# Loading w2 two rows per partition, and reading w1's columns with a step of two

## The chip, the cores and the metric

The kernel runs on one core of one Trainium2 chip. The metric is the device time of one execution in microseconds (us). Several executions are timed; most of one kernel agree within about 1%, and now and then one is much longer at a lower granted TensorE clock. Such slow runs are left out of every ratio; the medians and ranges given below are over all runs of a kernel, slow ones included. A profile is one execution recorded by the hardware profiler. Its span is some 1.6 us shorter than the device time of the same run (167.6 against 169.21 us for the kernel before).

## The reference, cut to what matters

A sparse attention is followed by a mixture of experts with one expert for each batch entry.

```python
batch, n_heads, seq, head_dim = (4, 8, 768, 64)
B, S, D, E, F = (4, 768, 512, 8, 1024)
...
pooled = x.mean(axis=1)
e_idx = np.argmax(pooled @ w_gate, axis=1)
...
h = np.maximum(x[mask] @ w1[e], 0.0)      # w1[e]: 512 x 1024
out[mask] = gate_w * (h @ w2[e])          # w2[e]: 1024 x 512
```

Which expert a batch entry takes is known only when its attention is done. Then its w1 and w2 are loaded, as fp32 in HBM and bf16 in SBUF, while TensorE works on the attention of the next entry.

## The kernel before

The hidden dimension F = 1024 is cut into eight tiles `ft` of 128 columns of w1. Each tile is a 128-column weight load for each of the four row blocks `dt` of w1. w1 arrives in `CHUNKS[b]` pieces: four for batch entry 0, so that TensorE can begin when the first quarter of the columns has landed.

```python
CHUNKS = (4, 1, 4, 2)
...
sb["w1"] = moe_pool.tile([128, NDT, F], BF16, name="w1_sb")     # NDT = 4
sb["w2"] = moe_pool.tile([128, NFT, DM], BF16, name="w2_sb")    # NFT = 8
...
def w1f(c):
    fs = slice(c * F // CHUNKS[b], (c + 1) * F // CHUNKS[b])
    nc.gpsimd.dma_start(
        sb["w1"][:, :, fs],
        moe_w1[ds(sb["e"], 1)].rearrange("o (dt p) f -> p (o dt) f", p=128)[:, :, fs],
    )

def w2f():
    nc.gpsimd.dma_start(
        sb["w2"], moe_w2[ds(sb["e"], 1)].rearrange("o (ft p) d -> p (o ft) d", p=128)
    )
...
def h(ft, c0, c1):
    def mm():
        ...
        for dt in range(NDT):
            nc.tensor.matmul(
                ps["t"][:, 0 : c1 - c0],
                lhsT=sb["w1"][:, dt, ft * 128 : (ft + 1) * 128],
                rhs=sb["xT"][:, dt, c0:c1],
                start=(dt == 0), stop=(dt == NDT - 1),
            )
```

The order of instructions on each engine is worked out beforehand by the program's own scheduler from estimated durations.

The softmax here doesn't subtract the row's maximum and nothing guards it: scores larger than these inputs give would overflow.

## Time and profile before

| | kernel before |
|---|---|
| device time, median (range) | 169.25 us (168.56 to 172.78), 3 runs |
| profiled span | 167.6 us |
| TensorE busy | 158.1 us, 94% |
| mean granted clock | 1.000 |
| TensorE idle between 38 and 99 us | 3.2 us |

In the profile, PE is the TensorE matmul, PEld its weight load, POOL is GpSimd, ACT ScalarE and DVE VectorE. "L973" is a line of the kernel. In a timeline line, the bracket at the end is the idle time of that engine before the group, and what ended it.

### The profile page before, as it was taken

What the parts mean: (1) busy time and instruction counts of PE and PEld (TensorE: products, weight loads), DVE (VectorE), ACT (ScalarE), POOL (GpSimd) and SP (SyncE); (2) the same over time, 40 slices, a digit from 0 to 9 for tenths busy, and PEclk for the clock granted to TensorE, in tenths of its full rate; (3) what the DMA queues carried; (4) which work ended last, traced back from release to release, by engine and by line L of the source; (5) the groups of instructions that cost most, each with busy time, mean ns of one, the idle gap of its engine ahead of it and who ended that gap; (6) DMA issues with size and microseconds to landing.
All of it is one profiled execution on the core that took longest, in us unless ns stands there. A gap on an engine that the chain in (4) does not pass through costs nothing.

```text
span 167.6 us, 4958 instructions
## 1 busy us (share of the span) xinstructions
PE 158.1 (94%) x2085; PEld 91.2 (54%) x2085; DVE 99.6 (59%) x237; ACT 106.7 (64%) x196; POOL 63.7 (38%) x90
## 2 busy tenths in 40 slices
PE   6999999989899999899999889999999999999992
PEld 2446767745566564455666544555556544565451
DVE  5798785988996676799675787989542000000000
ACT  3455755476778889596877584559778534565342
POOL 6999937337940483951013893000002300000000
PEclk9999999999999999999999999999999999999999
DMA  4999999956999999699999999995300999900063
GB/s 100 204 235 223 176 247 215 188 101 82 150 198 206 243 217 194 105 207 272 233 261 246 216 199 199 221 242 161 132 2 4 142 185 200 348 4 0 11 241 125
DMA packets 24902, 29.06 MB, mean 173 GB/s; under 512 B 3856, under 2 KB 19472, under 8 KB 24880
## 3 DMA queue, kind: packets, MB, share of 16 engines
q0 software_dynamic: 18352, 20.58, 73.0%
q1 hardware_dynamic: 6528, 8.17, 15.8%
q8 instruction: 16, 0.26, 0.7%
q14 instruction: 6, 0.05, 0.1%
HBM read 35.67 MB, written 6.29 MB: 250 GB/s over the span
## 4 chain that ended last, share of the span: by engine, by line
PE 49%; DMA 26%; DVE 10%; issue 5%; POOL 4%; ACT 2%; POOLq 1%; ACTq 0%
DMA q_nat<-in_q_dram 13%; PE hps L1006 12%; PE hps L973 9%; DMA k_nat<-in_k_dram 8%; PE third L1006 7%; DMA v_f<-in_v_dram 5%; PE third L973 5%; DVE vblk L374 3%; PE sc L642 3%; PE ops L680 2%; PE ops L492 2%; PE tps L587 2%; PE sc L631 2%; PE third L1099 1%; DVE xs L706 1%
## 5 line engine op out<-in xcount | busy, mean ns | idle before, releaser
L263 POOL DMA_DIRECT2D v_f<-in_v_dram x30 | 25.2, 850 | 27.3 <-DMA w_sb<-in_moe_w_dram 19.6
L973 PE MATMUL hps<-xT_b,w_sb 128*128 128x512 bf16 (+1 forms) x172 | 33.3, 328 | 2.0 <-ACT hT_sb L984 1.5
L653 ACT ACTIVATE aT<-sc 128x768 bf16<-128x768 f32 x32 | 25.9, 810 | 14.2 <-PE sc L642 14.1
L973 PEld LDWEIGHTS <-w_sb 128*128 128x128 bf16 x256 | 23.1, 98 | 15.3 <-issue 1.5
L1006 PEld LDWEIGHTS <-hT_sb 128*128 128x128 bf16 x200 | 18.7, 98 | 19.9 <-issue 0.4
L1006 PE MATMUL hps<-w_sb,hT_sb 128*128 128x512 bf16 (+1 forms) x128 | 29.0, 373 | 0.2 <-ACT hT_sb L984 0.2
L984 ACT ACTIVATE hT_sb<-hps 128x512 bf16<-128x512 f32 (+1 forms) x43 | 20.2, 491 | 4.5 <-PE hps L973 4.3
L886 POOL DMA_DIRECT2D w_sb<-in_moe_w_dram x11 | 8.2, 753 | 31.8 <-PE hps L973 27.0
L1099 PE MATMUL third<-idle_in 128*128 128x512 bf16 (+3 forms) x61 | 17.0, 386 | 1.6 <-DVE warm L277 1.6
L1016 ACT ACTIVATE o_sb<-hps,gcol 128x512 f32<-128x512 f32 (+1 forms) x16 | 10.8, 673 | 10.3 <-PE hps L1006 9.3
L973 PE MATMUL third<-xT_b,w_sb 128*128 128x256 bf16 (+1 forms) x84 | 16.9, 324 | 0.0
L1006 PE MATMUL third<-w_sb,hT_sb 128*128 128x512 bf16 (+1 forms) x72 | 16.2, 368 | 0.0
L706 DVE TENSOR_TENSOR xs<-ops,rv 128x384 bf16<-128x384 f32 x28 | 15.6, 557 | 1.0
L724 ACT ACTIVATE xT_b<-tps 128x768 bf16<-128x768 bf16 x16 | 13.0, 810 | 3.2 <-PE tps L716 3.0
L657 DVE TENSOR_TENSOR aT<-aT,mask 120x768 bf16<-120x768 bf16 x22 | 12.0, 553 | 2.8 <-ACT aT L653 2.7
L581 DVE COPY kT<-kps 128x960 bf16<-128x960 bf16 (+1 forms) x18 | 12.7, 743 | 1.7 <-PE kps L561 1.7
L680 PEld LDWEIGHTS <-aT 120*64 120x64 bf16 (+1 forms) x384 | 8.7, 110 | 8.9 <-issue 5.0
L984 ACT ACTIVATE hT_sb<-third 128x256 bf16<-128x256 f32 (+1 forms) x21 | 10.1, 483 | 3.9 <-PE third L973 3.8
L705 DVE RECIPROCAL rv<-ops 128x6 f32<-128x6 f32 x28 | 5.4, 194 | 11.4 <-PE ops L680 8.9
L450 POOL CAST v_h<-v_f 128x768 bf16<-128x768 f32 x12 | 9.9, 836 | 5.9 <-DMA v_f<-in_v_dram 5.7
L1016 ACT ACTIVATE o_sb<-third,gcol 128x512 f32<-128x512 f32 (+1 forms) x9 | 6.0, 663 | 8.4 <-PE third L1006 8.4
L612 DVE TENSOR_REDUCE kmx<-kT 128x24 bf16<-128x768 bf16 x12 | 11.3, 939 | 0.0
(83 smaller groups left out, 209.5 us busy)
## 6 DMA issues: line engine op xcount, KB each, us to landing
out_dram<-o_sb SPq DMA_DIRECT2D x23, 256.0 KB, 5.1
v_f<-in_v_dram POOLq DMA_DIRECT2D x30, 192.0 KB, 9.7
w_sb<-in_moe_w_dram POOLq DMA_DIRECT2D x5, 1024.0 KB, 13.9
k_nat<-in_k_dram POOLq DMA_DIRECT2D x6, 384.0 KB, 8.4
q_nat<-in_q_dram POOLq DMA_DIRECT2D x6, 384.0 KB, 10.1
w_sb<-in_moe_w_dram POOLq DMA_DIRECT2D x8, 256.0 KB, 7.7
vblk<-vblk SPq DMA_DIRECT2D x12, 89.4 KB, 5.3
w_sb<-in_moe_w_dram POOLq DMA_DIRECT2D x2, 512.0 KB, 6.4
```

The lines of the kernel that those rows point to most:

```text
L263: eng.dma_start(v_f[:, :, h, :], v[b, h].rearrange("(j p) d -> p j d", p=128))
L581: nc.vector.tensor_copy(kdst, win)
L653: nc.scalar.activation(aT, sb["sc"][:, :, 0 : NH * QB], ACT.Exp, scale=SCALE)
L657: nc.vector.tensor_tensor(out=aT[0:NR], in0=aT[0:NR], in1=mask[:, hf * NH : (hf + 1) * NH, :] .rearrange("p j c -> p (j c)") .unsqueeze(1) ...
L680: nc.tensor.matmul(ops[(j % 2) * QB : (j % 2 + 1) * QB, hh, jj // 2, :], lhsT=aT[0:rows, hh, jj * QB : (jj + 1) * QB], rhs=vb[0:rows, pr, ...
L706: nc.vector.tensor_tensor(out=sb["xs"][pr][:, hf * NS : (hf + 1) * NS, :, :].rearrange("p s h d -> p h s d"), in0=ops[:, :, :, 0:D], in1=r ...
L724: nc.scalar.activation(sb["xT"][:, pr, :].rearrange("p (j e g) -> p j e g", e=QB // G, g=G), sb["xps"].rearrange("p j g e -> p j e g"), AC ...
L973: nc.tensor.matmul(ps["t"][:, 0 : c1 - c0], lhsT=sb["w1"][:, dt, ft * 128 : (ft + 1) * 128], rhs=sb["xT"][:, dt, c0:c1], start=(dt == 0), ...
L984: nc.scalar.activation(sb["hT"][:, ft, c0:c1], ps["t"][:, 0 : c1 - c0], ACT.Relu)
L1006: nc.tensor.matmul(ps["t"][:, 0:n], lhsT=sb["hT"][:, ft, st * 128 : (st + 1) * 128], rhs=sb["w2"][:, ft, c0:c1], start=(ft == 0), stop=(ft ...
L1016: nc.scalar.activation(ps["o"][:, 0:n], ps["t"][:, 0:n], ACT.Copy, scale=sb["gcol"][:, 0:1])
L1099: nc.tensor.matmul(idle[:, 0:c], lhsT=idle_in[:, 0:128], rhs=idle_in[:, 0:c], start=True, stop=True)
```

## The change

The intent is longer DMA packets. If a partition holds two neighbouring rows of w2, one packet covers 2 x 512 fp32 values, 4 KB, in place of 2 KB, and there are half as many. The rows then lie in another order over partitions, so the hidden units must too. Tile `ft` takes every second column of a block of 256 columns of w1.

```diff
         def w2f():
             nc.gpsimd.dma_start(
-                sb["w2"], moe_w2[ds(sb["e"], 1)].rearrange("o (ft p) d -> p (o ft) d", p=128)
+                sb["w2"].rearrange("p (c i) d -> p c (i d)", i=2),
+                moe_w2[ds(sb["e"], 1)].rearrange("o (c p i) d -> p (o c) (i d)", p=128, i=2),
             )
...
-                        lhsT=sb["w1"][:, dt, ft * 128 : (ft + 1) * 128],
+                        lhsT=sb["w1"][:, dt, ft // 2 * 256 : (ft // 2 + 1) * 256].rearrange(
+                            "p (f i) -> p i f", i=2
+                        )[:, ft % 2, :],
```

## The prediction

> **What bounds the kernel now.** I read the page's engine totals first, then the busy time of each engine by stretch, then the chain of work that ended last, then the few stretches in which TensorE stood still, and last the DMA traffic.
>
> ```profile
> PE 158.1 (94%) x2085; PEld 91.2 (54%) x2085; DVE 99.6 (59%) x237; ACT 106.7 (64%) x196; POOL 63.7 (38%) x90
> ...
> q0 software_dynamic: 18352, 20.58, 73.0%
> ```
>
> TensorE is busy 158.1 of 167.6 us, so 9.5 us are idle. By stretch (columns: window, its length, busy us and instructions of each engine, granted clock, DMA share, GB/s):
>
> ```profile
> 8.00:38.00 30.00, 28.77 (x546) 18.83 (x544) 25.21 (x59) 17.70 (x30) 19.95 (x28) 1.00 1.07 196
> 38.00:99.00 61.00, 57.82 (x916) 34.31 (x915) 47.96 (x108) 46.75 (x89) 32.04 (x41) 1.00 1.10 202
> 99.00:143.00 44.00, 44.00 (x476) 23.84 (x475) 21.13 (x50) 27.10 (x51) 5.21 (x7) 1.00 0.84 152
> ```
>
> The last row matters most: from 99 to 143 us TensorE never stops, so no earlier weight can help there; only work handed to it before 99 us can. Between 38 and 99 us it is idle for 3.2 us. The TensorE timeline shows where (start, us, what, idle before it and its releaser):
>
> ```profile
> 43.40 1.04 PE L973 MATMUL hps<-xT_b,w_sb 128*128 128x512 bf16 x4 [0.49 <-DMA w_sb<-in_moe_w_dram]
> ...
> 67.79 0.38 PE L909 MATMUL ops<-grec,ones_row 1*128 1x1 f32 x2 [1.15 <-DVE grec L906]
> ...
> 97.14 0.60 PE L973 MATMUL hps<-xT_b,w_sb 128*128 128x256 bf16 x4 [1.54 <-ACT hT_sb L984]
> ```
>
> The first is the first piece of w1 of batch 0, which the change does not move. The other two are what is at stake. The chain, in order of time, says what lies behind them (start, us, what):
>
> ```profile
> 42.60 13.38 DMA k_nat<-in_k_dram
> ...
> 56.27 8.53 DMA v_f<-in_v_dram
> ...
> 69.71 21.82 DMA q_nat<-in_q_dram
> ...
> 94.04 0.84 POOL v_h L450
> 94.91 0.85 ACT vblk L372
> 95.77 0.85 ACT vblk L372
> 96.62 0.48 ACT hT_sb L984
> ```
>
> It runs through GpSimd's DMA queue. In that queue w2 of batch 0 stands ahead of the k, q and v that batch 2 needs (the 13.38 us), and w2 of batch 1 ahead of those of batch 3 (the 21.82 us). v that lands late is cast late (POOL L450), the in-order ScalarE and VectorE sit in front of that cast (ACT L372; at 66 us DVE L374), and TensorE waits. So two of the four w2 transfers are on the path. The other two (batch 2 from about 106 us, batch 3 from about 138 us) lie beside a TensorE that is full; batch 3's w2 is first used near 154 us.
>
> **What the Trainium skill says.** "DMA: Bandwidth & Descriptors", section "Why small descriptors are slow (HBM only)": each packet pays a fixed cost of about three cycles, 27% at 256 bytes; longer packets pay it less often. Its section "Where 436 GB/s comes from" puts a ceiling of 435 GB/s on 16 engines. The trace agrees that little is left. w2 now moves as packets of 2,048 bytes of fp32 in, 1,024 of bf16 out; w1 of batch 1, loaded whole, already has the length that w2 would get, 4,096 in and 2,048 out. Two stretches in which each has the queue practically to itself:
>
> ```profile
> 48.50:51.50 3.00, 3.00 (x45) 2.04 (x44) 2.77 (x7) 2.16 (x6) 0.49 (x1) 1.00 1.24 209
> 71.50:72.50 1.00, 1.00 (x11) 0.34 (x10) 1.00 (x3) 0.95 (x4) 1.00 (x2) 1.00 1.18 211
> ```
>
> The last column counts bytes written: 209 GB/s for the short packets, 211 for the long. Read in fp32 that is 418 and 422 GB/s, both near the page's 435.
>
> "TensorE: Matmul & The Clock Gate", section "Weight-path perf modes": a weight load of 128 columns that are not fp32 is done in a fast mode, in four chunks of 32 columns "packed or strided", for column steps up to 1,024. A step of two should keep it. The trace shows that the mode is on (TensorE weight-load groups; the number after the comma is ns of one):
>
> ```profile
> L973 PEld LDWEIGHTS <-w_sb 128*128 128x128 bf16 x256 | 23.1, 98 | 15.3 <-issue 1.5 <-DMA w_sb<-in_moe_w_dram 0.6
> ...
> L680 PEld LDWEIGHTS <-aT 120*64 120x64 bf16 x288 | 6.5, 110 | 8.0 <-issue 4.9 <-DVE xs L706 1.3 <-DVE vblk L520 0.8
> ...
> L492 PEld LDWEIGHTS <-bind 64*32 64x32 bf16 x48 | 2.8, 92 | 0.5 <-issue 0.3
> ```
>
> 128 columns take 98 ns, less than the 110 ns of 64. No strided load is in this trace, so the step itself is untested here.
>
> **The change part by part.**
>
> 1. w2's packets. Each w2 has 128 x 8 = 1,024 packets now and 128 x 4 = 512 after; bytes are the same. Four transfers lose 4 x 512 = 2,048 packets. Time of one w2 alone on the queue: 1,048,576 bytes / 209 GB/s = 5.02 us now, / 211 = 4.97 us after: 0.05 us less. While output stores share the engines (part of batch 1's w2), the saving may be larger; I allow 0.05 to 0.25 us there. Two on the path: 0.1 to 0.3 us, I take 0.2.
>
> 2. Issue on GpSimd. A w1 issue with 512 packets takes 0.75 us and a w2 issue with 1,024 takes 0.90 us in the median (w2 rows of that line: 899/902/1067 ns). So w2 should come down to 0.75, 0.15 us less. But k, q and v behind it stand in a queue that is already full for 20 us, so this lies beside the transfer: I count 0.05 us on the path.
>
> 3. Room in the queue. GpSimd stands still before v's issues until earlier transfers land: 19.6 us in 5 waits for w_sb. Half as many packets should let it issue one or two v transfers earlier. They still run behind w2 in the same queue, and the last issues still wait for w2 and k to land, so the last v lands no earlier for it: 0.
>
> 4. w1's weights with a step of two: 256 loads in number as before. If the fast mode stays: 98 ns, 0. If it falls off: by the 92 and 110 ns above, one column costs (110 - 92)/32 = 0.56 ns, so 128 would take 110 + 64 x 0.56 = 146 ns (an estimate). The narrow matmuls of L973 (256 columns) follow each other at (0.60 - 0.273)/3 = 0.109 us, where 0.273 is the length of one. Transposes of 128 columns, each with its own 128-column load, go at
>
> ```profile
> 61.50 0.50 PE L716 MATMUL tps<-identb,xs 128*128 128x128 bf16 x6
> ```
>
> (0.50 - 0.22)/5 = 0.056 us with 98 ns loads, so loads overlap each other and their length is mostly latency. A slow load would add some 48 ns of it and still fit in 109: 0.
>
> 5. Nothing else: the moving operands, the order of instructions on each engine, PSUM and the evictions are as before (w2 sits in the tile in the same shape, with its rows permuted as hT's partitions are).
>
> Sum: 0.2 + 0.05 = 0.25 us less. 169.25 - 0.25 = 169.0 us.
>
> **Rivals.**
>
> - The per-packet cost counts in full. The records of single packets have a median of 60, 98 and 173 ns for 512, 1,024 and 2,048 written bytes: some 23 ns fixed. If packets ran one after the other, w2 would go from 1,024 x 98/16 = 6.27 us to 512 x 173/16 = 5.54 us, 0.74 less, 1.5 us for the two: 167.8 us. For it: both stalls (1.15 and 1.54 us) are large enough to give that. Against it: the DMA share of 1.24 says that packets overlap, and the rate of 209 against 211 GB/s is measured, not inferred.
> - The long packets overlap less or starve the output stores: w1 of batch 1 has a share of 1.18 instead of 1.24. If w2 came out 0.5 us longer each, the time would be about 170.0.
> - The strided load costs TensorE. If loads could not overlap and took 146 ns, the 128 narrow matmuls of L973 would each lose 146 - 109 = 37 ns: 4.7 us, all on a full TensorE, 174.0 us. The L716 spacing speaks against it; nothing in this trace rules out a load that is slow in throughput.
> - A larger gain is barred: both stalls gone entirely would be 1.15 + 1.54 = 2.7 us, 166.6 us or 1.6%, still short of 2%.
>
> **Range and chances.** The three earlier runs lie between 168.56 and 172.78, with the profiled one at 169.21, so most of the range is scatter around 169.0; the first rival stretches it down, the second up. 168.0 to 170.1 us. Faster by over 2% would need more than the two stalls: 0.01. Slower by over 2% needs the strided load to fail, or a slow draw: 0.04. Within 2%: 0.95.
>
> **What would show it.** The software queue should have 16,304 packets instead of 18,352 and the same 20.58 MB; its share falls, by the packet medians, by 4 x (6.27 - 5.54)/167.6 = 1.8 points to about 71.2%. w2's issue on GpSimd near 0.75 us. The waits of v's issues for w_sb in two or three pieces instead of five, with a similar sum. The loads of L973 at 98 ns, their matmuls still 0.109 and 0.217 us apart. The two stalls before L909 near 67 us and L973 near 97 us shorter by 0.1 to 0.3 us together, and TensorE without a gap from then to 143 us. I am wrong if L973's loads are over 110 ns and its matmuls spread, if a stall on w_sb appears where none was, or if a stall shrinks by a microsecond, which would mean that packets cost more than the rates show.

## More of the kernel before

The waits on semaphores (counters that a finished instruction or transfer raises and that others wait for) are not written in the program. The framework puts them in from what each instruction reads and writes.

## The result, and the profile after

The changed kernel took 173.99 us in the median of four runs (173.55 to 175.55), against 169.37 us for four runs of before. The ratio is 1.03, with a 95% interval of 1.0226 to 1.0374. Ratios here are the mean time of one kernel's fast runs over that of the other's from the same rounds, so they are not quite the ratio of the medians. The profiled run was the longest, 175.55 us with a span of 174.0; a second profile, e7 below, has 171.5.

The page after, with its busy time, the clock by slice, and the software queue:

```profile
PE 158.2 (91%) x2057; PEld 92.1 (53%) x2085; DVE 101.2 (58%) x237; ACT 106.9 (61%) x196; POOL 63.2 (36%) x90
...
PEclk9999999999957999999999999999999999999999
...
q0 software_dynamic: 16304, 20.58, 68.9%
```

TensorE is as busy as before (158.2 us), but the span is 6.3 us longer, so it stands still longer. In two slices near 50 us the granted clock is lower. The software queue moves the same 20.58 MB in 2,048 packets fewer, as intended. What TensorE waited for, after (us in total, times, longest):

```profile
PE hps L974 <- DMA w_sb<-in_moe_w_dram: 6.0, 1, 6.0
...
PE hps L974 <- ACT hT_sb L987: 1.3, 1, 1.3
```

Before, the same first row had 0.5 us. One wait for w1 or w2 is now 6 us long. The weight loads show where it starts (timeline of PEld after):

```profile
43.20 0.10 PEld L974 LDWEIGHTS <-w_sb 128*128 128x128 bf16 x1 [0.47 <-DMA w_sb<-in_moe_w_dram]
48.82 0.14 PEld L974 LDWEIGHTS <-w_sb 128*128 128x128 bf16 x2 [5.52 <-issue]
```

The first load of batch 0's first group, row block 0, goes at 43.20 us. The second, row block 1, comes 5.6 us later. The profile calls the idle time before it "issue", which means that it names no releaser. In the kernel before, all four loads of this group go together, the first two 15 ns apart (timeline of PEld before):

```profile
43.40 0.54 PEld L973 LDWEIGHTS <-w_sb 128*128 128x128 bf16 x4 [0.62 <-DMA w_sb<-in_moe_w_dram]
```

Each load has its matmul. The record of the group's first matmul is missing from the trace after, so that timeline has three:

```profile
48.85 1.44 PE L974 MATMUL hps<-xT_b,w_sb 128*128 128x512 bf16 x3 [5.98 <-DMA w_sb<-in_moe_w_dram]
```

The chain that ended last names the transfer (start, us, what):

```profile
40.77 7.95 DMA w_sb<-in_moe_w_dram
...
48.85 1.44 PE hps L974 x3
```

What was issued at 40.8 us is w1's fourth and last piece, and it landed at 48.7. The trace also has a new instruction on the queue of weight loads, one that only waits for semaphores (minimum, median, maximum ns; first and last start in us):

```profile
L974 PEldq EVENT_SEMAPHORE  x2: 51/51/51, 48.7 to 124.9; - x2
```

The one at 48.7 us waits for pieces three and four, and the second load itself for piece two. In the kernel before, the group waited for the first piece's semaphore alone. The one at 124.9 us belongs to batch 2; its pieces had landed by 117.1 us, so there the wider wait costs nothing. The waiting is followed by a slow stretch (window, length, busy us of the five engines, granted clock, DMA share, GB/s; after):

```profile
43.30:48.80 5.50, 0.00 (x0) 0.00 (x0) 2.54 (x4) 0.85 (x2) 3.81 (x5) 0.91 1.28 185
48.80:55.00 6.20, 6.15 (x52) 3.02 (x53) 2.54 (x5) 2.34 (x4) 1.65 (x2) 0.53 1.17 204
```

TensorE does nothing for 5.5 us and then runs at a mean clock of 0.53 until 55 us. The matmuls of 512 columns start 0.425 us apart in that stretch, where they start 0.216 apart otherwise. "TensorE: Matmul & The Clock Gate", section "Part 1: The HAM clock gate", says that the clock falls to one half after an idle window of about 3.4 us and comes back after a busy one. The long waits agree: the half clock runs from 47.85 to 54.67 us here and for 3.41 us in e7, each time after TensorE had stood still for the 3.4 us before. Other traces do not: in e1, e3, e6, e8 and e11 six stalls of 1.0 to 2.3 us were also followed by half clock (3.41 or 6.83 us of it), though TensorE was busy for 1.2 to 2.6 of the 3.4 us before the fall, while other stalls, up to the 1.8 us in e4, were not. What decides between these is not shown.

Both traces have 2,085 weight loads in the same order. The start of each one after, minus the start of the same one before, gives the account:

| place in the kernel before | shift after | shift e7 (second profile) |
|---|---|---|
| 42.5 us, before the first w1 group | -0.05 us | -0.37 us |
| 43.41 us, second load of that group | +5.41 | +4.38 |
| 55 us, clock back at full | +7.79 | +5.66 |
| 66 us | +7.80 | +5.66 |
| 70 us, past the old stall before L909 | +6.57 | +4.44 |
| 99 us, past the old stall before L973 | +6.34 | +3.91 |
| 164 us, last store's matmul | +6.35 | +3.92 |

The wait costs 5.5 us (4.7 in e7), the half clock another 2.4 (1.3). Of this 1.2 us come back at 67 us. The kernel before had stood still there for 1.15 us because v came late, and with TensorE itself late, v is no longer what it waits for. Another 0.2 to 0.5 us come back near 97 us. From 99 us on nothing changes.

### The profile page after: what moved, and what is told of

It is laid out like the page before. It is cut to its first block, busy times and chain, and to the rows that moved or that the text cites. A ratio compares the mean times of both kernels' runs of the same rounds, so it can differ in the third digit from the quotient of the medians.

```text
span 174.0 us, 4932 instructions
## 1 busy us (share of the span) xinstructions
PE 158.2 (91%) x2057; PEld 92.1 (53%) x2085; DVE 101.2 (58%) x237; ACT 106.9 (61%) x196; POOL 63.2 (36%) x90
## 3 DMA queue, kind: packets, MB, share of 16 engines
q0 software_dynamic: 16304, 20.58, 68.9%
## 4 chain that ended last, share of the span: by engine, by line
PE 55%; DMA 17%; DVE 15%; issue 5%; POOL 3%; ACT 2%; POOLq 1%; ACTq 0%
PE hps L974 14%; DMA q_nat<-in_q_dram 13%; PE hps L1009 12%; PE third L1009 6%; PE third L974 6%; DMA w_sb<-in_moe_w_dram 5%; PE ops L680 3%; PE sc L642 3%; DVE vblk L374 3%; DVE kT L581 2%; PE tps L716 2%; PE tps L587 2%; PE sc L631 2%; DVE xs L706 1%; DVE vblk L313 1%
## 5 line engine op out<-in xcount | busy, mean ns | idle before, releaser
L974 PE MATMUL hps<-xT_b,w_sb 128*128 128x512 bf16 (+1 forms) x164 | 34.3, 337 | 7.6 <-DMA w_sb<-in_moe_w_dram 6.0
L974 PEld LDWEIGHTS <-w_sb 128*128 128x128 bf16 x256 | 23.6, 100 | 21.4 <-issue 8.2
L263 POOL DMA_DIRECT2D v_f<-in_v_dram x30 | 25.4, 854 | 26.2 <-DMA w_sb<-in_moe_w_dram 17.5
L1009 PE MATMUL hps<-w_sb,hT_sb 128*128 128x512 bf16 (+1 forms) x121 | 28.4, 372 | 0.7 <-ACT hT_sb L987 0.2
L1009 PE MATMUL third<-w_sb,hT_sb 128*128 128x512 bf16 (+1 forms) x68 | 15.5, 367 | 0.4 <-issue 0.3
L657 DVE TENSOR_TENSOR aT<-aT,mask 120x768 bf16<-120x768 bf16 x22 | 12.8, 587 | 2.8 <-ACT aT L653 2.8
L642 PE MATMUL sc<-qT,kT 64*128 64x64 bf16 x384 | 11.5, 194 | 0.0
L642 PEld LDWEIGHTS <-kT 64*128 64x128 bf16 x384 | 7.6, 96 | 7.1 <-issue 5.3
```

The source lines that it names most:

```text
L263: eng.dma_start(v_f[:, :, h, :], v[b, h].rearrange("(j p) d -> p j d", p=128))
L642: nc.tensor.matmul(sc[:, hh, jj * QB : (jj + 1) * QB], lhsT=sb["kT"][pr][rs, j, :], rhs=sb["qT"][pr][rs, j, :], start=not add_shut, stop=n ...
L657: nc.vector.tensor_tensor(out=aT[0:NR], in0=aT[0:NR], in1=mask[:, hf * NH : (hf + 1) * NH, :] .rearrange("p j c -> p (j c)") .unsqueeze(1) ...
L974: nc.tensor.matmul(ps["t"][:, 0 : c1 - c0], lhsT=sb["w1"][:, dt, ft // 2 * 256 : (ft // 2 + 1) * 256].rearrange("p (f i) -> p i f", i=2)[: ...
L1009: nc.tensor.matmul(ps["t"][:, 0:n], lhsT=sb["hT"][:, ft, st * 128 : (st + 1) * 128], rhs=sb["w2"][:, ft, c0:c1], start=(ft == 0), stop=(ft ...
```

## The experiments

My theory after seeing the two traces was this. When the framework asks which transfers a read must wait for, it compares a contiguous read with each transfer's pieces exactly, but takes a strided view by its outer limits. Piece c of w1 covers columns 256c to 256c+255 of all four row blocks of 1,024 columns, so its outer limits run from 256c to 3,072 + 256c + 255. A strided read in row block 1 (1,024 to 1,278) lies within the outer limits of all four pieces. One in row block 0, columns 0 to 254, lies within those of the first piece only. The rivals were that strided weight loads are themselves slow, and that the long w2 packets hurt the queue.

e1, e6, e4 and e2 ran on one chip with five rounds, e3, e5 and e7 on one with three, and e8, e9 and e11 on another with three to five.

### e1: the change, with w1 stored piece by piece

```diff
+            sb["w1c"] = sb["w1"].rearrange("p dt f -> p (dt f)").rearrange(
+                "p (c dt f) -> p c dt f", c=CHUNKS[b], dt=NDT)
...
-                sb["w1"][:, :, fs],
+                sb["w1c"][:, c, :, :],
...
+                per = NFT // CHUNKS[b]
-                        lhsT=sb["w1"][:, dt, ft // 2 * 256 : (ft // 2 + 1) * 256].rearrange(
+                        lhsT=sb["w1c"][:, ft // per, dt, ft % per // 2 * 256 : (ft % per // 2 + 1) * 256].rearrange(
```

> The changed kernel with w1's tile stored piece by piece, so that each of batch 0's four w1 transfers fills one unbroken stretch of a partition; the strided weights and the long w2 packets stay. Theory (the wait): a strided view was taken to touch every transfer whose outer limits it crosses, so the second weight load waited for all four; here it crosses one only. The 5.5 us stall and the half clock after it go, the first L974 group runs near 43.2 us without a gap inside, clock 1.0, and the time is 168.6 to 169.6 us, ratio to before 0.995 to 1.002. Rival (strided loads themselves cost TensorE): it stays at 172 to 174. Rival (long w2 packets hurt the queue): it stays above 171. The sum of my prediction, a gain of 0.25 us, would show as 0.9985.

Measured: correct, 169.56 us median (168.81 to 170.25), ratio 1.0012 (0.995 to 1.0074). The loss is gone although every w1 load is strided and every w2 packet is long. The timeline of e1's TensorE:

```profile
44.60 0.81 PE L978 MATMUL hps<-xT_b,w_sb 128*128 128x512 bf16 x3 [0.16 <-issue]
```

There is no wait inside the group. It ran at 44.6 us, while the last packets of w1's fourth piece were written at 48.6. The profiled run reached this place 1 us late because of a 1.0 us stall at 31.7 us before attention matmuls, with 3.4 us of half clock after it (mean clock 0.99, where I had expected 1.0). Such a stall between 31 and 35 us is in the profiles of e1, e3, e5, e6, e8 and e11.

### e6: the kernel before, with w1 stored piece by piece

The same layout with contiguous weights and short w2 packets.

> The kernel before with the same piece-by-piece w1 tile, contiguous weights and short w2 packets: the control for e1. Theory: the kernel before did not suffer from the wait, so nothing changes, ratio 0.998 to 1.002. Rival: if the layout of the tile alone speeds w1's transfer or moves a wait, this differs from 1 as much as e1 does.

Measured: correct, 169.75 us (168.85 to 170.3), ratio 1.0023 (0.9958 to 1.0087). The ratio is just above the expected 1.002, and its interval includes 1. The layout by itself changes nothing that these runs resolve, so e1's recovery is not a gain of the layout that hides a loss of the stride.

### e4: w2's long packets alone

```diff
-                sb["w2"], moe_w2[ds(sb["e"], 1)].rearrange("o (ft p) d -> p (o ft) d", p=128)
+                sb["w2"].rearrange("p (c i) d -> p c (i d)", i=2),
+                moe_w2[ds(sb["e"], 1)].rearrange("o (c p i) d -> p (o c) (i d)", p=128, i=2),
```

> Wrong result on purpose: only w2's packets are two rows long, w1 is read as before, so w2's rows do not match the hidden units. Theory: no wait is added, ratio 0.996 to 1.001 (a gain of 0.1 to 0.3 us of 169), w2 issue 0.75 us, 16,304 packets. Rival (the fixed 23 ns of a packet count in full): 1.5 us less, ratio 0.991. Rival (long packets hurt): above 1.005.

Measured: wrong result; 169.37 us (168.79 to 171.63), ratio 0.9997 (0.9933 to 1.0061). The long packets neither hurt nor help the time measurably. The interval ends at 0.9933, so the 0.991 of the rival that counts each packet's fixed cost in full is outside it, if narrowly. The stretch in which batch 0's w2 has the queue to itself, e4:

```profile
48.50:51.50 3.00, 3.00 (x50) 2.03 (x46) 2.87 (x7) 2.16 (x5) 0.82 (x1) 1.00 1.13 214
```

It moves 214 GB/s where the kernel before moved 209, which would make one w2 of 1,048,576 bytes 0.12 us shorter (4.90 us in place of 5.02). But in the same window the other profiles have 212 with short packets (e6) and 213 (e1) and 210 (after) with long ones, so a gain of this size is not told from scatter.

### e2: one strided view added to the kernel before

```diff
                 ps["t"] = moe_bank(ps["n"])
+                if b == 0 and ft == 0 and c0 == 0:
+                    nc.tensor.matmul(
+                        ps["t"][:, 0:1],
+                        lhsT=sb["w1"][:, 1, 0:256].rearrange("p (f i) -> p i f", i=2)[:, 0, :],
+                        rhs=idle_in[:, 0:1], start=True, stop=True)
                 for dt in range(NDT):
```

> The kernel before plus one matmul of one column whose weights are a strided view of w1 of batch 0, row block 1, put ahead of the first group; everything else is contiguous, and the result is right because the group starts its sum afresh. Theory (the wait): this single strided view is enough to wait for all four w1 transfers; stall near 5.5 us at 43 us, half clock after it, total 173 to 174.5 us, ratio 1.022 to 1.037. Rival (the 256 strided loads cost): one load costs nothing, ratio 1.00.

Measured: correct, 175.16 us (173.89 to 176.96), ratio 1.0336 (1.0252 to 1.0419). The time is above the expected 173 to 174.5 us, the ratio within what was expected. One strided load out of 257 brings the whole loss:

```profile
48.55 0.16 PE L973 MATMUL hps<-idle_in,w_sb 128*128 128x1 bf16 x1 [5.93 <-DMA w_sb<-in_moe_w_dram]
```

### e8: the same, in row block 0

```diff
-                        lhsT=sb["w1"][:, 1, 0:256].rearrange("p (f i) -> p i f", i=2)[:, 0, :],
+                        lhsT=sb["w1"][:, 0, 0:256].rearrange("p (f i) -> p i f", i=2)[:, 0, :],
```

> As e2, but the strided one-column matmul reads row block 0 of w1 in place of row block 1. Theory (outer limits): block 0, columns 0 to 255, ends before the second transfer's first element, so its outer limits cross the first transfer alone; no wait is added, ratio 0.995 to 1.005. Rival (any strided view waits for every transfer into the tile): ratio 1.022 to 1.037 as e2.

Measured: correct, 169.43 us (167.99 to 171.91), ratio 0.9946 (0.9889 to 1.0004). The ratio is just under the expected 0.995 to 1.005, and far from the rival's. Its profile fell on a run of 171.91 us that counts as slow, so only its order of events is read:

```profile
44.67 0.18 PE L973 MATMUL hps<-idle_in,w_sb 128*128 128x1 bf16 x1
44.92 0.81 PE L981 MATMUL hps<-xT_b,w_sb 128*128 128x512 bf16 x3
```

The strided load and the group behind it wait for nothing, while w1's second, third and fourth pieces landed only at 47.4, 48.7 and 50.0 us. So it is not any strided view of the tile that waits for all transfers. It depends on where the view lies, as the outer limits say.

### e3: w1's step alone

The w1 part of the diff without the w2 part.

> Wrong result on purpose: only w1's columns are read with a step of two, w2 is loaded as before. Theory (the wait): the whole loss is here, ratio 1.022 to 1.037, the 5.5 us stall at 43 us. Rival (long w2 packets are the cause): ratio 1.00.

Measured: wrong result; 175.7 us (174.39 to 187.18), ratio 1.0333 (1.0241 to 1.0425). The whole loss belongs to the w1 half of the change. In the profiled run the wait was 4.2 us rather than 5.5, since that run came to the group 2.6 us late, after the stall at 32 us and the half clock that followed it.

### e5 and e7: work to do during the wait, and the change again

```diff
                 ps["t"] = moe_bank(ps["n"])
+                if b == 0 and ft == 0 and c0 == 0:
+                    for _ in range(26):
+                        nc.tensor.matmul(
+                            ps["t"], lhsT=idle_in[:, 0:128], rhs=idle_in, start=True, stop=True)
                 for dt in range(NDT):
```

> The changed kernel with 26 idle matmuls of 512 columns put ahead of batch 0's first w1 group, so that TensorE has work while it waits for all of w1. 26 x 0.216 us = 5.6 us, about the wait. Theory: the wait stays but the clock does not fall, so the 2.35 us that the half clock took between 48.8 and 55 us are saved: 171.2 to 172.2 us, ratio 1.010 to 1.020, mean clock 1.0. Rival (the clock falls for another reason, or the loss is elsewhere): as the changed kernel, 1.025 to 1.03.

> The changed kernel unaltered, on the same chip as the two others, for comparison: ratio 1.022 to 1.037, clock 0.98.

Measured: e5 was correct, 173.66 us (172.17 to 187.07, the last a slow run), ratio 1.0183 (1.0105 to 1.0262). e7 took 173.7 us (173.11 to 174.87), ratio 1.0274 (1.0205 to 1.0343). The ratio of e5 is within what was expected, but its median is not (nor is that of its three fast runs, 172.94), and the two intervals overlap, so the timing alone does not settle it. The trace of e5 does, in two windows, the wait and what follows:

```profile
44.90:50.30 5.40, 5.39 (x25) 2.45 (x25) 2.73 (x4) 1.13 (x2) 4.00 (x5) 1.00 1.29 189
50.30:56.00 5.70, 5.54 (x74) 3.21 (x74) 3.14 (x7) 3.74 (x8) 1.38 (x2) 1.00 1.17 205
```

The clock stays at 1.00. From the second load to 55 us the shift against before goes from +7.08 to +6.90, so nothing is added, where the changed kernel added 2.4 and e7 1.3 us. The fall of the clock is a consequence of the wait and costs 1.3 to 2.4 us, depending on the run.

### e9 and e11: batch 1's w2 issued behind batch 3's v

The stall at 97 us, which my prediction wanted to shorten, comes from v standing behind w2 in the queue. w2 is not needed so early, so I moved it.

```diff
-        w2 = add("POOL", 0.8, [], w2f, dma=6.3, after=w1[-1:])
+        if b in (1,):
+            w2 = lambda o: add("POOL", 0.8, [], w2f, dma=6.3, after=w1[-1:] + o)
+        else:
+            w2 = add("POOL", 0.8, [], w2f, dma=6.3, after=w1[-1:])
...
             vl, rest = load_next(nxt + 1, last_T[b], casts, order_pool)
+            if b in (1,):
+                ...
+                w = (w[0], w[1](order_pool[:]), w[2])
```

> e1 (changed kernel, w1 stored piece by piece) with batch 1's w2 issued behind batch 3's v instead of ahead of it. w2 of batch 1 is first used near 101 us and landed near 88; v of batch 3 landed near 95 and holds up TensorE for 1.2 to 1.5 us at 97. Expected if that stall is the queue's: v some 5 us earlier, stall gone, w2 landing near 95, ratio to before 0.990 to 0.996. Rival: the program's own scheduler orders the engines anew from the changed list, and what it gains there it loses elsewhere: 0.997 to 1.01.

> The kernel before with the same late issue of batch 1's w2 and nothing else. Same expectation as e9, ratio 0.990 to 0.996: the order of the queue, not the length of the packets, is what the stall at 97 us depends on. Rival: 0.997 to 1.01, the new order of the engines gives it back.

Measured: both correct; e9 170.22 us (169.56 to 171.29), ratio 1.007 (1.0024 to 1.0116); e11 171.69 us (170.23 to 182.61), ratio 1.0105 (1.005 to 1.016). The rival held, though e11 lies just past its 1.01. In e9 the old stall has shrunk to 0.80 us at 92.5 us, but the scheduler had ordered the engines anew, and 1.2 us earlier a new stall of 1.41 us behind VectorE ends:

```profile
91.30 0.38 PE L680 MATMUL ops<-vblk,aT 120*64 120x65 bf16 x12 [1.41 <-DVE aT L657]
```

No version is shown to beat the kernel before. That a queue order alone, with the engines' order unchanged, would help was not tried.

## Why the prediction was wrong

I predicted 169.0 us in 168.0 to 170.1 and gave slower by over 2% a chance of 0.04. It came out 3% slower.

**The step that failed** is number 5, "Nothing else: the moving operands, the order of instructions on each engine, PSUM and the evictions are as before", together with the reading that the first of the three stalls "is the first piece of w1 of batch 0, which the change does not move". The order of instructions is indeed as before; the waits between them are not. The second weight load now waits for the fourth piece of w1 in place of the first. In the profile after that is 5.5 us of waiting and 2.4 of half clock, less the 1.2 and 0.2 that come back; in e7 it is 4.7 and 1.3, less 1.2 and 0.5. e3 puts the loss into the w1 half, e2 shows that one strided view is enough, e8 that it depends on where the view lies, and e1 that storing the pieces unbroken removes it with the change otherwise kept. That the framework compares outer limits is inferred from these four; its code was not looked at. My list of signs of error did name "a stall on w_sb appears where none was", but I gave it no mechanism and no chance.

**Step 1, w2's packets, was neither shown nor refuted.** 0.05 us was expected for a transfer alone; e4's window gives 0.12, within the scatter of the other profiles. The sum of my prediction, 0.25 us or 0.15% of the time, is smaller than the 0.6% to which e4 and e1 resolve. The two stalls that should have been shorter by 0.1 to 0.3 us together came to 1.8 and 1.1 us in e4's trace, 2.9 against 2.7 before, so the sign that I named did not show either. The rival of 1.5 us is excluded by e4. One reading in the prediction was loose: the 435 GB/s that I set beside 418 and 422 is given by the page for the ports on the SBUF side, where 209 and 211 were written; the 418 and 422 are bytes read from HBM.

**Step 2, the issue on GpSimd, was right in its duration.** I expected 0.75 us; its 0.05 us on the path is too small to be seen. The row for the w2 issues, after (minimum, median, maximum ns):

```profile
L892 POOL DMA_DIRECT2D w_sb<-in_moe_w_dram x4: 752/757/845, 41.7 to 136.6; - x4
```

**Step 3, room in the queue, was wrong in its sign to watch for.** GpSimd's waits before v for w_sb came to 17.5 us in 6 pieces after, and 18.3 in 5 in e4, against 19.6 in 5. I had expected two or three pieces. That the last v lands no earlier for it fits e4's unchanged time, but was not measured apart.

**Step 4, the strided load, was right.** All loads of w1, after (minimum, median, maximum ns):

```profile
L974 PEld LDWEIGHTS <-w_sb x256: 96/98/151, 43.2 to 159.6; 128*128 128x128 bf16 x128
```

The median is 98 ns, as with contiguous columns; the 151 ns belong to the half clock. At full clock the matmuls start 0.109 and 0.216 us apart, as before. A step of two leaves the load time as it was, which agrees with the page cited in the prediction. It is a coincidence that the rival in which these loads are slow came to 174.0 us. A right figure for a cause that the trace refutes is no confirmation.

## What to carry to other kernels

When a tile is filled by several transfers and a change alters only the form in which it is read, ask what the read now waits for. Compare the waits of the first readers before and after, ahead of any sum of transfer times. Where a strided view is wanted, lay the tile out so that each transfer fills one unbroken stretch: here that cost nothing (e6) and took the whole loss away (e1). A wait on TensorE can cost more than its length: in the profiles here every one of over 4 us was followed by half clock (after, e7, e2, e3), and so were some of 1.0 to 2.3 us.

## What the Trainium skill lacked or had wrong

- No page has it: a strided view of a tile that several DMAs fill can be made to wait for all of them, though it reads what one of them wrote. Here that wait was 4.7 to 5.5 us (e7, after), and a single view brings it (e2, 5.93 us idle before it).
- "Perfetto Trace Analysis", section "DMA Optimizations", says that batching small transfers into larger ones, from 2 KB to 4 KB or 8 KB, can improve throughput dramatically. That section does not say what happens where only the packets of a large transfer grow. Here, from 2 KB to 4 KB read per packet in transfers of 1 MB written, 209 and 212 GB/s (before, e6) became 210 to 214 (after, e1, e4), 2.4% at most.
- "TensorE: Matmul & The Clock Gate", section "LDWEIGHTS (loading the stationary operand)", gives columns/1.2 ns as the time of a load, 107 for 128 columns, 53 for 64 and 27 for 32. In the profile before, a load of 128 columns takes 98 ns, one of 64 columns 110 and one of 32 columns 92, so the recorded duration does not follow this formula.
- The same page's section "Weight-path perf modes" agrees for a step of two: 98 ns strided and contiguous.
- The clock section of the same page, cited above, ties the fall of the clock to an idle window of about 3.4 us. Six stalls of 1.0 to 2.3 us (e1, e3, e6, e8, e11) were followed by half clock too, and others up to 1.8 us (e4) were not.
